# A long convolution and two gated layers on one core: PSUM laid out anew between stages, one product kept in PSUM, one fold on GpSimd

## The chip, the cores and the metric

The kernel runs on one core of a Trainium2 chip. The metric is device time in microseconds, the median of several runs. The engines are named as the profile names them: PE is TensorE (PEld is its weight load), DVE is VectorE, ACT is ScalarE, POOL is GpSimd, SP is SyncE, which here only issues DMAs. SBUF and PSUM are the two on-chip memories; PSUM has eight banks of 512 fp32 values in each of 128 partitions.

## The reference

Everything is fp32. A filter is made from `pos_emb`, `w1` and `w2`, windowed, and convolved along the sequence (12480 positions, 128 channels) with x times v, through a Fourier transform; the result, times x, goes through two two-layer networks.

```
h_filt = (relu(pos_emb @ w1) @ w2) * exp(-0.01 * pos)
y = irfft(rfft(x * v, 2S) * rfft(h_filt, 2S))[:S];  x = x * y
r = relu(x @ w_in);          x = (r * r) @ w_out
h = x @ w_in2;               out = (max(h, 0) + alpha * min(h, 0)) @ w_out2
```

## The kernel before

The transform of length 110 x 229 is done as two small ones with matmuls (`dfa` of 110, `dfb` of 229 folded to 115 rows). The channels are worked in two halves: h = 0, whose spectrum U(0) stands in the gaps of the big SBUF buffer G, and h = 1, whose spectrum U(1) fills the buffer R2. The work runs in stages, each a set of generators whose steps are interleaved by `run` (each generator has a weight, and the one that is least far along takes its next step). The code is written in this order, and each engine works through its own queue in it, waiting on semaphores:

- First stages (0 to 62.8 us): the filter (`z_stage`, `ar_stage`).
- Stage one (62.8 to about 136 us): `u_stage(0)` with `r_stage`. A step k of `u_stage` loads x and v, multiplies them on GpSimd two steps' worth ahead (`prep`, L251, two multiplies), transforms them (`u_mm_a`, L267 to L272) and, one step later, transforms again (`u_mm_b`, L280 to L287): two odd matmuls go to one PSUM bank and are copied to SBUF by ScalarE (L283), one even matmul goes to another bank, and VectorE writes even plus odd and even minus odd (L287, the two folds). `r_stage` makes the filter's tiles r and spills them.
- Stage two (about 136 to 236 us): `u_stage(1)`, 17 steps, with `p_stage(0)`, 14 steps.
- Stage three (236 to 299.4 us): `p_stage(1)`, 14 steps, with `b_stage(0)` (the inverse transform of half 0, L353, copied out by ScalarE, L361).
- After it: `b_stage(1)` (which reads U(1)), `y_stage`, and from 383 us on the two networks (`moe`), to the end. While these run, the networks' weights are decoded (`weights`, L437 to L454; L437 reads a PSUM bank and writes a PSUM bank).

A step of `p_stage` is a complex product of the spectrum with the filter for eight columns. For each of the parts c = 0 and c = 1, eight matmuls (L329) write a PSUM bank H, and VectorE multiplies U by H into the SBUF tile T (L334; half 0 in two instructions of 128 and 896 elements, half 1 in one of 1024). A is T's part 0, B its part 1. VectorE takes A's real half minus B's imaginary half (L341); one step later `finish` runs on GpSimd: A's imaginary half plus B's real half (L308), and the sums and differences that go back to U (L314). In the last step of each half VectorE does one of these two (also L314). All operands of L341, L308 and L314 are in SBUF. T is a ring of two.

PSUM is laid out once: eight tiles of one bank. Rings hand them out: `r_a` banks 0 and 1 (L267), `r_b` banks 2 to 4 (even and odd of `u_mm_b`), `r_h` banks 5 to 7 (H, and `r_stage`), `r_ab` banks 0 to 4 (`b_stage(0)`), `r_y` banks 0 to 5.

Of the kernel before, what the change touches and what calls it, by code (L numbers as in the profile page):

```python
# [9 lines left out]
F32 = mybir.dt.float32  # L10
# [5 lines left out]
ALU = mybir.AluOpType  # L16

S, D, F, FF = 12480, 128, 64, 2048
# [4 lines left out]
K2 = 2 * KA  # L23
HB = (NB + 1) // 2
# [7 lines left out]
DG = 4  # L32
# [18 lines left out]
def ring_of(pool, n, shape, dtype, name):  # L51
    return Ring(pool.tile(shape, dtype, name=f"{name}{i}") for i in range(n))
# [3 lines left out]
def kernel(  # L56
# [21 lines left out]
    nc = tc.nc  # L78
    PSUM = bass.MemoryType.PSUM
# [2 lines left out]
    dram = ctx.enter_context(tc.tile_pool(name="dram", bufs=1, space=bass.MemoryType.DRAM))  # L82
    s_g = ExitStack()
    p_g = s_g.enter_context(tc.tile_pool(name="p_g", bufs=1, side="right"))
    psum = ctx.enter_context(tc.tile_pool(name="psum", bufs=1, space=PSUM))
    banks = [psum.tile([128, 512], F32, name=f"bank{i}") for i in range(8)]
    r_any, r_a, r_b, r_h = Ring(banks), Ring(banks[0:2]), Ring(banks[2:5]), Ring(banks[5:8])
    r_ab, r_y = Ring(banks[0:5]), Ring(banks[0:6])

    def bank(ring, p, *dims):  # L90
        n = 1
        for d in dims:
            n *= d
        names = "uvwxyz"[:len(dims)]
        return ring()[:p, :n].rearrange(
            f"p ({' '.join(names)}) -> p {' '.join(names)}", **dict(zip(names, dims))
        )
# [160 lines left out]
        return bass.AP(tensor=v.tensor, offset=v.offset + HB - 1, ap=st)  # L258

    a_t = {}  # L260

    def u_mm_a(k):
        u = [t[:NA, :, 0:HB] for t in x_ring[k % NX][1:]]
# [10 lines left out]
    def u_mm_b(k):  # L274
        h, g = divmod(k, NG)
        a = a_t.pop(k)
        po = bank(r_b, HB, DG, 2, KA)
        pe = bank(r_b, HB, DG, K2)
        ao = a[:, 1].rearrange("p d (k c) -> p d k c", c=2)
        nc.tensor.matmul(po[:, :, 0], lhsT=nsinb, rhs=ao[:, :, :, 1])  # L280
        nc.tensor.matmul(po[:, :, 1], lhsT=sinb, rhs=ao[:, :, :, 0])
        t = t_ring[k % 2][:HB]
        nc.scalar.copy(out=t.rearrange("p d (k c) -> p d k c", c=2), in_=po.rearrange("p d c k -> p d k c"))  # L283
        nc.tensor.matmul(pe, lhsT=cosb, rhs=a[:, 0])  # L284
        u = U(h, 2 * DG * g, 2 * DG).rearrange("p (d s) k -> p d s k", s=2)
        for s, op in ((0, ALU.add), (1, ALU.subtract)):
            nc.vector.tensor_tensor(out=u[:, :, s], in0=pe, in1=t, op=op)  # L287

    def u_stage(h):
        for k in range(h * NG, (h + 1) * NG + 1):  # L290
            if k < (h + 1) * NG:
                load(k + NX - 1)
                u_mm_a(k)
                prep(k + NX - 3)
            if k > h * NG:
                u_mm_b(k - 1)
            yield
# [3 lines left out]
    p_order += [(j + nj - 6) % nj for j in range(nj)]  # L301

    def p_stage(h, t_ring, r_ring):
        late = []

        def finish(n, j, A, B):
            last = n % nj == nj - 1
            nc.gpsimd.tensor_tensor(out=A[:, :, :, 1], in0=A[:, :, :, 1], in1=B[:, :, :, 0], op=ALU.add)  # L308
            for x0, m in parts(h):
                y = A[:, x0:x0 + m].rearrange("p (d s) k c -> p d s (k c)", s=2)  # L310
                u = U(h, x0, m).rearrange("p (d s) k -> p d s k", s=2)[:, :, :, 8 * j:8 * j + 8]
                for s, op in ((0, ALU.add), (1, ALU.subtract)):
                    eng = nc.vector if last and s == 0 else nc.gpsimd
                    eng.tensor_tensor(out=u[:, :, s], in0=y[:, :, 0], in1=y[:, :, 1], op=op)  # L314

        for n in range(h * nj, (h + 1) * nj):
            j = p_order[n]
            m = p_order[min(n + 2, 2 * nj - 1)]
            if m not in r_t:
                del r_t[p_order[n - 1]]  # L320
                r_t[m] = r_ring()
                nc.sync.dma_start(out=r_t[m].rearrange("p q c k -> p (q c k)"), in_=spill[m])
            r = r_t[j]
            T = t_ring()
            for c in range(2):
                H = bank(r_h, HB, DH, 2, 2, 2)
                for q in range(2):
                    for s in range(2):
                        nc.tensor.matmul(  # L329
                            H[:, :, s, q], lhsT=r[:, q, 2 * s + c], rhs=w2_sb[:, h * D:(h + 1) * D]  # L330
                        )
                hv = H.rearrange("p d s q r -> p (d s) (q r)")
                for x0, m in parts(h):
                    nc.vector.tensor_tensor(  # L334
                        out=T[:, c, x0:x0 + m],
                        in0=U(h, x0, m)[:, :, 8 * j:8 * j + 8].rearrange("p x (k c) -> p x k c", c=2),
                        in1=hv[:, x0:x0 + m].unsqueeze(3).to_broadcast([HB, m, 4, 2]),
                        op=ALU.mult,
                    )
            A, B = T[:, 0], T[:, 1]  # L340
            nc.vector.tensor_tensor(out=A[:, :, :, 0], in0=A[:, :, :, 0], in1=B[:, :, :, 1], op=ALU.subtract)  # L341
            if late:
                late.pop()()
            late.append(lambda n=n, j=j, A=A, B=B: finish(n, j, A, B))
            yield
        late.pop()()

    def b_stage(h, alone):
        for g in range(NG):
# [64 lines left out]
    def run(*gens):  # L414
        live = [[g, n, i * 1e-6] for i, (g, n) in enumerate(gens)]
        while live:
            live.sort(key=lambda e: e[2])
            e = live[0]
            try:
                next(e[0])  # L420
                e[2] += 1.0 / e[1]
            except StopIteration:
                live.remove(e)
# [109 lines left out]
    n = NCH * NT  # L533
    i = j = 0
# [140 lines left out]
    with tc.manual_schedule():  # L675
        with ExitStack() as st:
            late = st.enter_context(tc.tile_pool(name="late", bufs=1))
            w2_sb = late.tile([128, 2 * D], F32, name="w2_sb")
            dfa = late.tile([NA, K2], F32, name="dfa")
            dfa_f = late.tile([NA, K2], F32, name="dfa_f")  # L680
            r_ring = ring_of(late, 3, [128, 2, 4, HB], F32, "r")
            with tc.tile_pool(name="early", bufs=1) as early:
                run((z_stage(*load_first(early)), 1))
                run((ar_stage(early), 1))
            with tc.tile_pool(name="rt", bufs=1) as rt:
                run((u_stage(0), NG + 1), (r_stage(rt, r_ring), KP))
            big = st.enter_context(tc.tile_pool(name="tt", bufs=1))
            tt = ring_of(big, 2, [HB, 2, D, 4, 2], F32, "T")
            p0, q0 = p_stage(0, tt, r_ring), p_stage(1, tt, r_ring)
            run((u_stage(1), NG + 1), (p0, nj + 1))  # L690
            run((q0, nj + 3), (b_stage(0, False), NG))
        wa = ctx.enter_context(tc.tile_pool(name="wa", bufs=1))
        wst = ctx.enter_context(tc.tile_pool(name="wst", bufs=1))
        decode = weights(wst)
# [179 lines left out]
```

## Time and profile before

| | |
|---|---|
| median of 3 runs | 1478.89 us (1477.95 to 1481.53) |
| profiled execution | 1478.57 us, span 1476.8 us |
| PE busy in the span | 1441.3 us (98%) |
| DVE, POOL, ACT busy | 80%, 71%, 65% |
| mean granted TensorE clock | 0.992 |

The page's shares are means over stages with different limits. From 306 us on PE is busy in every slice, and the chain that ended last runs through PE's matmuls; the change touches none of that work. What it touches lies between 62 and 300 us, so the rows below are taken from there. A row of a timeline merges instructions that follow each other on an engine; behind it stands, in brackets, the idle time before it and who ended it.

### The profile page before, as it was taken

Reading aid. Unit: us, or ns where it says so; the run is one execution under the profiler, and the core shown is the slowest. Engines: PE = TensorE matmul, PEld = TensorE weight load, DVE = VectorE, ACT = ScalarE, POOL = GpSimd, SP = SyncE. Lnnn points to the kernel's source line nnn. Section 1 sums busy time; section 2 is a strip of 40 time slices with the busy share of each in tenths; the row PEclk is TensorE's granted clock in tenths of the full one; section 3 lists DMA queues with packets and bytes.
Section 4 is the critical chain, followed back from the end, with each engine's and each line's share of the span. In section 5 each row is a group of like instructions: output and inputs, shape, how many; then the busy total and the mean of one; then the engine's idle time right before and its main releaser. Section 6 shows DMA issues by size and latency. Waiting matters only on the chain.

```text
span 1476.8 us, 23093 instructions
## 1 busy us (share of the span) xinstructions
PE 1441.3 (98%) x7634; PEld 1231.4 (83%) x7634; DVE 1174.6 (80%) x1852; ACT 966.9 (65%) x1857; POOL 1042.9 (71%) x851
## 2 busy tenths in 40 slices
PE   8999888889999999999999999999999999999998
PEld 8989778789888888888888888888888888888887
DVE  5978998769778877777777777777777787777998
ACT  5333112262588777777777777777777777777776
POOL 2245998944677777777777777777777777777766
PEclk9999989999999999999999999999999999999999
DMA  9388922239600000000000000000000000000000
GB/s 285 94 217 230 211 84 78 65 106 278 205 22 8 1 8 8 1 8 8 8 8 8 7 2 8 7 8 8 8 1 8 8 8 8 8 8 1 15 15 14
DMA packets 73869, 76.83 MB, mean 52 GB/s; under 512 B 6739, under 2 KB 65428, under 8 KB 73364
## 3 DMA queue, kind: packets, MB, share of 16 engines
q1 hardware_dynamic: 72650, 71.12, 17.4%
q0 software_dynamic: 688, 3.93, 0.8%
q8 instruction: 60, 0.98, 0.3%
q14 instruction: 62, 0.50, 0.1%
q10 hardware_dynamic: 409, 0.29, 0.1%
HBM read 58.41 MB, written 16.92 MB: 51 GB/s over the span
## 4 chain that ended last, share of the span: by engine, by line
PE 89%; POOL 5%; DVE 3%; issue 2%; DMA 1%; ACT 0%; POOLq 0%; DVEq 0%; ACTq 0%
PE bank L565 24%; PE bank L566 24%; PE bank L567 24%; PE bank L267 3%; PE bank L353 2%; PE bank L168 2%; PE bank L407 2%; PE bank L406 2%; DVE R L205 2%; PE bank L223 2%; POOL R L314 2%; POOL T L308 2%; PE bank L284 1%; PE bank L329 1%; PE bank L280 1%
## 5 line engine op out<-in xcount | busy, mean ns | idle before, releaser
L618 POOL TENSOR_TENSOR g<-R,g 128x500 fp32r<-128x500 f32 (+1 forms) x598 | 776.9, 1320 | 279.6 <-ACT g L607 204.2
L600 DVE SCALAR_TENSOR_TENSOR R<-bank,e 128x500 f32<-128x500 f32 (+1 forms) x800 | 531.4, 674 | 172.3 <-POOL g L618 95.4
L607 ACT CAST g<-R 128x500 fp32r<-128x500 f32 (+1 forms) x800 | 466.3, 604 | 32.3 <-DVE R L600 28.4
L585 ACT ACTIVATE e<-bank 128x500 f32<-128x500 f32 (+1 forms) x400 | 234.7, 587 | 165.2 <-PE bank L567 162.1
L590 DVE TENSOR_SCALAR e<-bank,alpha 128x500 f32<-128x500 f32 (+1 forms) x266 | 195.3, 734 | 50.4 <-PE bank L567 50.1
L618 DVE TENSOR_TENSOR g<-R,g 128x500 fp32r<-128x500 f32 (+1 forms) x202 | 158.2, 784 | 0.0
L566 PE MATMUL bank<-g,w_o 128*128 128x500 f32 (+1 forms) x400 | 155.7, 389 | 0.4 <-POOL g L618 0.4
L567 PE MATMUL bank<-g,w_o 128*128 128x500 f32 (+1 forms) x400 | 155.5, 389 | 0.0
L566 PE MATMUL bank<-x,w_i 128*128 128x500 f32 (+1 forms) x400 | 155.4, 388 | 0.0
L565 PE MATMUL bank<-x,w_i 128*128 128x500 f32 (+1 forms) x400 | 155.2, 388 | 0.0
L565 PE MATMUL bank<-g,w_o 128*128 128x500 f32 (+1 forms) x400 | 155.0, 388 | 0.0
L567 PE MATMUL bank<-x,w_i 128*128 128x500 f32 (+1 forms) x400 | 155.0, 387 | 0.0
L567 PE MATMUL bank<-g,w_o0b 128*128 128x500 f32 (+1 forms) x350 | 136.4, 390 | 0.0
L566 PE MATMUL bank<-g,w_o0b 128*128 128x500 f32 (+1 forms) x350 | 136.3, 389 | 0.0
L565 PE MATMUL bank<-g,w_o0b 128*128 128x500 f32 (+1 forms) x350 | 135.7, 388 | 0.0
L251 POOL TENSOR_TENSOR G<-G 110x460 f32<-110x460 f32 x64 | 73.9, 1174 | 86.7 <-DMA G<-in_vs_dram 49.3
L587 ACT ACTIVATE e<-bank 128x500 f32<-128x500 f32 (+1 forms) x134 | 78.8, 588 | 39.3 <-PE bank L567 38.6
L588 ACT ACTIVATE e<-e,alpha 128x500 f32<-128x500 f32 (+1 forms) x134 | 95.6, 714 | 4.4
L566 PEld LDWEIGHTS bank<-x,w_i 128*128 128x128 f32 x400 | 75.1, 188 | 15.9
L566 PEld LDWEIGHTS bank<-g,w_o 128*128 128x128 f32 x400 | 75.2, 188 | 15.8 <-POOL g L618 0.8
L565 PEld LDWEIGHTS bank<-x,w_i 128*128 128x128 f32 x400 | 75.3, 188 | 15.6
L565 PEld LDWEIGHTS bank<-g,w_o 128*128 128x128 f32 x400 | 75.2, 188 | 15.4
(107 smaller groups left out, 2632.1 us busy)
## 6 DMA issues: line engine op xcount, KB each, us to landing
G<-in_vs_dram SPq DMA_DIRECT2D x64, 224.0 KB, 5.5
r<-spill SPq DMA_DIRECT2D x22, 460.0 KB, 4.2
G<-in_xs_dram SPq DMA_DIRECT2D x32, 224.0 KB, 5.4
spill<-r SPq DMA_DIRECT2D x14, 460.0 KB, 3.0
out_dram<-R SPq DMA_DIRECT2D x24, 250.0 KB, 2.0
R<-in_xt_dram SPq DMA_DIRECT2D x27, 218.0 KB, 3.8
s_w<-in_moe_w_in_dram SPq DMA_DIRECT2D x16, 256.0 KB, 3.4
s_w<-in_moe_w_out_dram SPq DMA_DIRECT2D x16, 256.0 KB, 3.6
```

What stands on the lines that cost most here:

```text
L251: nc.gpsimd.tensor_tensor(out=u[:, :, 0:HB], in0=u[:, :, 0:HB], in1=y, op=ALU.mult)
L267: nc.tensor.matmul(p[s][:, d], lhsT=u[s][:, d], rhs=dfa)
L565: nc.tensor.matmul(p, lhsT=wl, rhs=xh, start=first, stop=False)
L566: nc.tensor.matmul(p, lhsT=wh, rhs=xl, start=False, stop=False)
L567: nc.tensor.matmul(p, lhsT=wh, rhs=xh, start=False, stop=last)
L585: nc.scalar.activation(out=r, in_=p, func=ACTF.Relu)
L587: nc.scalar.activation(out=r, in_=p, func=ACTF.Relu, scale=-1.0)
L588: nc.scalar.activation(out=r, in_=r, func=ACTF.Copy, scale=alpha[:, t:t + 1])
L590: nc.vector.tensor_scalar(out=r, in0=p, scalar1=0.0, scalar2=alpha[:, t:t + 1], op0=ALU.min, op1=ALU.mult)
L600: nc.vector.scalar_tensor_tensor(out=g, in0=p, scalar=0.0, in1=r, op0=ALU.max, op1=op)
L607: nc.scalar.copy(out=gh, in_=g)
L618: eng.tensor_tensor(out=gl, in0=g, in1=gh.bitcast(F32), op=ALU.subtract)
```

## The change

- PSUM is laid out three times. `lay_banks` closes the pool of PSUM tiles and opens another: eight tiles for the first stages and stage one; then, for stages two and three, six tiles of one bank and one tile `wide` of two banks; then eight tiles again. In stages two and three `r_b` and `r_h` shrink from three banks to two, and `r_ab` from five to four.
- In `p_stage` the c = 1 product B is written to `wide` in PSUM instead of SBUF. The tile A alone is the ring of two in SBUF. Real and imaginary part are now both finished on VectorE (L356 of the new code), and GpSimd's addition L308 is gone. `finish` comes at the end of its own step instead of one step later.
- In `u_mm_b` the even matmul comes first. In stage two (h = 1) ScalarE copies its bank to a new SBUF tile `even`, and the second fold (even minus odd) goes to GpSimd; in stage one both folds stay on VectorE.

```diff
@@ lay_banks
+    def lay_banks(name, n):
+        s_psum.close()
+        pool = s_psum.enter_context(tc.tile_pool(name=name, bufs=1, space=PSUM))
+        tiles = [pool.tile([128, 512], F32, name=f"{name}{i}") for i in range(n)]
+        if n < 8:
+            tiles.append(pool.tile([128, (8 - n) * 512], F32, name=f"{name}_wide"))
+        return tiles
@@ u_mm_b
+        pe = bank(r_b, HB, DG, K2)
         po = bank(r_b, HB, DG, 2, KA)
-        pe = bank(r_b, HB, DG, K2)
+        nc.tensor.matmul(pe, lhsT=cosb, rhs=a[:, 0])
+        even = None
+        if h:
+            even = even_ring[0]()
+            nc.scalar.copy(out=even, in_=pe)
...
-        nc.tensor.matmul(pe, lhsT=cosb, rhs=a[:, 0])
...
-        for s, op in ((0, ALU.add), (1, ALU.subtract)):
-            nc.vector.tensor_tensor(out=u[:, :, s], in0=pe, in1=t, op=op)
+        nc.vector.tensor_tensor(out=u[:, :, 0], in0=pe, in1=t, op=ALU.add)
+        if h:
+            nc.gpsimd.tensor_tensor(out=u[:, :, 1], in0=even, in1=t, op=ALU.subtract)
+        else:
+            nc.vector.tensor_tensor(out=u[:, :, 1], in0=pe, in1=t, op=ALU.subtract)
@@ p_stage, finish
-            nc.gpsimd.tensor_tensor(out=A[:, :, :, 1], in0=A[:, :, :, 1], in1=B[:, :, :, 0], op=ALU.add)
@@ p_stage
-            T = t_ring()
-            for c in range(2):
+            A = t_ring()
+            B = wide[:HB].rearrange("p (x k c) -> p x k c", k=4, c=2)
+            for c, out_c in enumerate((A, B)):
...
-                        out=T[:, c, x0:x0 + m],
+                        out=out_c[:, x0:x0 + m],
...
-            A, B = T[:, 0], T[:, 1]
-            nc.vector.tensor_tensor(out=A[:, :, :, 0], in0=A[:, :, :, 0], in1=B[:, :, :, 1], op=ALU.subtract)
-            if late:
-                late.pop()()
-            late.append(lambda n=n, j=j, A=A, B=B: finish(n, j, A, B))
+            for c, op in ((0, ALU.subtract), (1, ALU.add)):
+                nc.vector.tensor_tensor(out=A[:, :, :, c], in0=A[:, :, :, c], in1=B[:, :, :, 1 - c], op=op)
+            finish(n, j, A)
@@ between stages
+            *few, wide = lay_banks("pb", 6)
+            r_a.items, r_b.items, r_h.items, r_ab.items = few[0:2], few[2:4], few[4:6], few[0:4]
-            tt = ring_of(big, 2, [HB, 2, D, 4, 2], F32, "T")
+            tt = ring_of(big, 2, [HB, D, 4, 2], F32, "T")
+            even_ring.append(ring_of(big, 2, [HB, DG, K2], F32, "even"))
...
+        banks = lay_banks("bank", 8)
+        r_y.items = banks[0:6]
```

GpSimd's queue at the start of stage two, before (T is the product's tile, G holds x, v and U(0)):

```order
L251 TENSOR_TENSOR G<-G 110x4x115 x42
L308 TENSOR_TENSOR T_1102<-T_1102 115x512
L314 TENSOR_TENSOR G<-T_1102 115x8x8 x2
L314 TENSOR_TENSOR G<-T_1102 115x56x8 x2
L251 TENSOR_TENSOR G<-G 110x4x115 x2
L308 TENSOR_TENSOR T_1103<-T_1103 115x512
L314 TENSOR_TENSOR G<-T_1103 115x8x8 x2
```

And now (L260 is `prep`, L328 the finish, L302 the new fold, which writes U(1) in R):

```order
L260 TENSOR_TENSOR G<-G 110x4x115 x40
L328 TENSOR_TENSOR G<-T_1113 115x8x8 x2
L328 TENSOR_TENSOR G<-T_1113 115x56x8 x2
L260 TENSOR_TENSOR G<-G 110x4x115 x2
L302 TENSOR_TENSOR R_78<-even_1115,G 115x4x112
L328 TENSOR_TENSOR G<-T_1114 115x8x8 x2
L328 TENSOR_TENSOR G<-T_1114 115x56x8 x2
```

A step now holds two multiplies, one fold and four finishing instructions, where it held L308, four finishing instructions and two multiplies; one pair of multiplies moved behind the first finish.

VectorE's queue in one step of stage two, before (L272 makes a, L287 is the two folds into R, L334 the products):

```order
L272 TENSOR_TENSOR G<-G,bank_70 115x4x112 x2
L287 TENSOR_TENSOR R_78<-bank_71,G 115x4x112 x2
L334 TENSOR_TENSOR T_1103<-G,bank_74 115x128
L334 TENSOR_TENSOR T_1103<-G,bank_74 115x896
L334 TENSOR_TENSOR T_1103<-G,bank_75 115x128
L334 TENSOR_TENSOR T_1103<-G,bank_75 115x896
L341 TENSOR_TENSOR T_1103<-T_1103 115x512
```

And now (L282 makes a, L300 is the one fold left, L349 the products, pb are the new banks):

```order
L282 TENSOR_TENSOR G<-G,pb_1104 115x4x112 x2
L300 TENSOR_TENSOR R_78<-pb_1105,G 115x4x112
L349 TENSOR_TENSOR T_1114<-G,pb_1107 115x128
L349 TENSOR_TENSOR T_1114<-G,pb_1107 115x896
L349 TENSOR_TENSOR pb_wide<-G,pb_1108 115x128
L349 TENSOR_TENSOR pb_wide<-G,pb_1108 115x896
L356 TENSOR_TENSOR T_1114<-T_1114,pb_wide 115x512 x2
```

One fold went to GpSimd and one L356 came; every instruction shown has a PSUM operand, where L341 had none.

PE's queue where stage one ends and stage two begins, with the semaphores that each row waits for, before (bank_69 and bank_70 are the ring `r_a`):

```order
L284 MATMUL bank_72<-G,dfb 115x448 [waits Activation_49]
L223 MATMUL bank_74<-dfb,R_78 128x115 x4
L267 MATMUL bank_69<-dfa,G 115x112 [waits DMAHW3_49,Pool_49]
L267 MATMUL bank_69<-dfa,G 115x112 x3
L267 MATMUL bank_70<-dfa,G 115x112 [waits DMAHW4_49,Pool_49]
```

And now:

```order
L296 MATMUL bank_72<-G,dfb 115x4x56
L232 MATMUL bank_74<-dfb,R_78 128x115 [waits Activation_49]
L232 MATMUL bank_74<-dfb,R_78 128x115 x3
L277 MATMUL pb_1103<-dfa,G 115x112 [waits DVE_49,DMAHW3_49,Activation_49,Pool_49]
L277 MATMUL pb_1103<-dfa,G 115x112 x3
```

The first matmul into the new layout waits for VectorE as well: for the last instruction that reads a tile of the old one (L239 of the new code, L230 of the old).

## Rows read from the trace of the kernel before

**Rows 1.** Busy time by stretch: us, us long, engines' busy us, PEclk, DMA share, GB/s.
```profile
100.00:136.00 36.00, 36.00 (x269) 31.80 (x268) 26.81 (x57) 13.08 (x29) 18.42 (x16) 1.00 0.84 218
136.00:236.00 100.00, 88.14 (x603) 76.68 (x602) 96.48 (x141) 17.38 (x33) 89.25 (x90) 0.91 0.57 136
236.00:299.40 63.40, 50.71 (x465) 48.54 (x463) 46.38 (x43) 17.46 (x32) 59.91 (x41) 1.00 0.27 83
300.00:306.00 6.00, 6.00 (x34) 6.00 (x34) 1.54 (x4) 1.75 (x4) 0.45 (x1) 0.52 0.58 94
```

**Rows 2.** Timeline of DVE and POOL in one step of stage two.
```profile
147.06 2.27 POOL L251 TENSOR_TENSOR G<-G 110x460 f32<-110x460 f32 x2
...
147.42 2.46 DVE L341 TENSOR_TENSOR T<-T 115x512 f32<-115x512 f32 x1
...
149.30 1.95 POOL L308 TENSOR_TENSOR T<-T 115x512 f32<-115x512 f32 x1
149.81 1.14 DVE L272 TENSOR_TENSOR G<-G,bank 115x448 f32<-115x448 f32 x2
...
150.87 1.15 DVE L287 TENSOR_TENSOR R<-bank,G 115x448 f32<-115x448 f32 x2
...
151.33 2.78 POOL L314 TENSOR_TENSOR G<-T 115x64 f32<-115x64 f32 x4
...
151.93 2.47 DVE L334 TENSOR_TENSOR T<-G,bank 115x128 f32<-115x128 f32 x4
...
154.04 2.31 POOL L251 TENSOR_TENSOR G<-G 110x460 f32<-110x460 f32 x2
```

**Rows 3.** Timeline where stage one ends and stage two begins.
```profile
136.73 1.77 PE L267 MATMUL bank<-dfa,G 110*115 110x112 f32 x16
...
137.67 0.39 DVE L230 TENSOR_TENSOR r<-bank,rt 128x230 f32<-128x230 f32 x1
...
142.18 0.69 DVE L341 TENSOR_TENSOR T<-T 115x512 f32<-115x512 f32 x1
```

**Rows 4.** Timeline from the end of stage two into stage three.
```profile
232.45 0.65 PE L280 MATMUL bank<-G,dfb 115*115 115x224 f32 x2 [1.60 <-DVE G L272]
...
233.34 0.91 PE L284 MATMUL bank<-G,dfb 115*115 115x448 f32 x2
233.38 1.42 DVE L314 TENSOR_TENSOR G<-T 115x64 f32<-115x64 f32 x2
...
235.97 2.35 DVE L334 TENSOR_TENSOR T<-R,bank 115x1024 f32<-115x1024 f32 x2
...
238.35 0.69 DVE L341 TENSOR_TENSOR T<-T 115x512 f32<-115x512 f32 x1
...
238.96 2.35 DVE L334 TENSOR_TENSOR T<-R,bank 115x1024 f32<-115x1024 f32 x2
```

**Rows 5.** Timeline of POOL in stage three.
```profile
243.39 1.52 POOL L308 TENSOR_TENSOR T<-T 115x512 f32<-115x512 f32 x1
244.98 2.95 POOL L314 TENSOR_TENSOR R<-T 115x512 f32<-115x512 f32 x2
```

**Rows 6.** Timeline of DVE and PE at the end of stage three.
```profile
290.48 4.92 PE L353 MATMUL bank<-dfb,G 115*112 115x116 f32 x48
...
298.64 0.69 DVE L314 TENSOR_TENSOR R<-T 115x512 f32<-115x512 f32 x1 [2.59 <-POOL T L308]
...
299.48 6.73 PE L353 MATMUL bank<-dfb,R 115*112 115x116 f32 x35 [4.08 <-DVE R L314]
```

**Rows 7.** Four lines' instructions: count, duration in ns (min/median/max), first and last start, form.
```profile
L205 DVE TENSOR_TENSOR R<-ar_p,bank x32: 911/937/953, 35.0 to 61.8; 115x448 f32<-115x448 f32 x32
L283 ACT COPY G<-bank x32: 532/532/533, 67.3 to 233.6; 115x448 f32<-115x448 f32 x32
L270 ACT COPY G<-bank x32: 532/532/533, 61.5 to 228.6; 115x448 f32<-115x448 f32 x32
L437 DVE TENSOR_SCALAR bank<-bank x32: 415/424/433, 304.3 to 487.4; 128x256 f32<-128x256 f32 x32
```

More of the change, by code (lines that the diff above doesn't have):

```diff
@@ L84 @@
     p_g = s_g.enter_context(tc.tile_pool(name="p_g", bufs=1, side="right"))
-    psum = ctx.enter_context(tc.tile_pool(name="psum", bufs=1, space=PSUM))
-    banks = [psum.tile([128, 512], F32, name=f"bank{i}") for i in range(8)]
+    s_psum = ctx.enter_context(ExitStack())
+    def lay_banks(name, n):
[6 more added lines that the diff above has]
+    banks = lay_banks("bank", 8)
     r_any, r_a, r_b, r_h = Ring(banks), Ring(banks[0:2]), Ring(banks[2:5]), Ring(banks[5:8])
-    r_ab, r_y = Ring(banks[0:5]), Ring(banks[0:6])
+    r_ab, r_y = Ring([]), Ring([])
     def bank(ring, p, *dims):
@@ L260 @@
     a_t = {}
+    even_ring = []
     def u_mm_a(k):
@@ L303, in p_stage, with finish @@
     def p_stage(h, t_ring, r_ring):
-        late = []
-        def finish(n, j, A, B):
+        def finish(n, j, A):
             last = n % nj == nj - 1
-            nc.gpsimd.tensor_tensor(out=A[:, :, :, 1], in0=A[:, :, :, 1], in1=B[:, :, :, 0], op=ALU.add)
             for x0, m in parts(h):
@@ L339, in p_stage @@
                     )
-            A, B = T[:, 0], T[:, 1]
-            nc.vector.tensor_tensor(out=A[:, :, :, 0], in0=A[:, :, :, 0], in1=B[:, :, :, 1], op=ALU.subtract)
-            if late:
-                late.pop()()
-            late.append(lambda n=n, j=j, A=A, B=B: finish(n, j, A, B))
+            for c, op in ((0, ALU.subtract), (1, ALU.add)):
+                nc.vector.tensor_tensor(out=A[:, :, :, c], in0=A[:, :, :, c], in1=B[:, :, :, 1 - c], op=op)
+            finish(n, j, A)
             yield
-        late.pop()()
     def b_stage(h, alone):
@@ L691 @@
             run((q0, nj + 3), (b_stage(0, False), NG))
+        banks = lay_banks("bank", 8)
+        r_y.items = banks[0:6]
         wa = ctx.enter_context(tc.tile_pool(name="wa", bufs=1))
```

## The prediction

> **What bounds the kernel now.** The page's chain of waits comes first: from 306 us on it is PE's matmuls, without a gap worth counting, and nothing there changes. So the question is how much earlier the work after stage three can start, and every microsecond won before 299.48 us [rows 6] should be one won at the end. The busy times by stretch come next [rows 1]. In stage one PE is busy 36.00 of 36 us, VectorE 26.81: PE bounds it. In stage two VectorE shows 96.48 and GpSimd 89.25 of 100, PE 88.14 at a granted clock of 0.91. In stage three GpSimd shows 59.91 of 63.4, PE 50.71, VectorE 46.38.
>
> The timeline of one step of stage two says what the two full engines really do [rows 2]. The step is 6.98 us long (L251 at 147.06 and 154.04). L341 takes 2.46 us, while the same instruction takes 0.69 where GpSimd is idle [rows 3, 4]. It starts at 147.42 inside GpSimd's pair of multiplies, which runs to 149.30, and ends 0.58 after that, at 149.88: it stood still until GpSimd was through. Then GpSimd's L308, issued at 149.30, takes 1.95 us instead of the 1.52 in stage three [rows 5]: it stood still until L341 was through. L272, L287 and L334, which take one operand from PSUM, run beside GpSimd at full pace: L334's four instructions take 2.47 beside L314. So VectorE's 96 us hold about 1.8 us of standing still in most of 14 steps, and the step's length is GpSimd's: 2.24 for L251, 2.03 for L308 (to the start of L314), 2.71 for L314. In stage three GpSimd alone sets the step: L308 and two L314, 1.52 + 2.95, about 4.5, times 14 is the stretch of 63.4 us.
>
> **Part by part. Stage two, GpSimd.** L308 goes; one fold of 115x448 comes. Its price is that of one multiply of 460 elements, 1.12 us [rows 2]; the bounds are 1.09 (448 of its 460 elements) and L308's 1.52. A step is then 2.24 + 1.12 + 2.71 = 6.1 us.
> **Stage two, VectorE.** One fold goes (0.53, half of the spacing 149.81 to 151.93 less L272's 1.06), L341 stays without its stall, and a second such instruction comes. Both L356 take one operand from PSUM, so by rows 2 they don't meet GpSimd. Two L341 follow at 0.61 (238.35 to 238.96) [rows 4], so the step is L282 1.06, L300 0.53, products 2.5, L356 1.22, together 5.3, with waits on its own results 5.4. GpSimd remains the longer one. Where L356 reads `wide` it takes every second fp32 value; no row shows VectorE reading PSUM so. The lower bound is 0.69; the upper one is L205, 937 ns for 448 elements, which jumps in SBUF and in PSUM [rows 7]: scaled from L334 (2.35 for 2048 elements, about 1.05 ns each and 0.14 fixed) it is 1.8 ns per element, so 1.05 us for 512. I take 0.69: L283 reads PSUM on ScalarE with jumps, and takes the same 532 ns as L270 without [rows 7]; L205's extra time can come from its SBUF side. The products that now go to PSUM: L437 writes PSUM at 424 ns for 256 elements [rows 7], which is 0.14 + 256 x 1.05 = 0.41 and so no dearer than SBUF; the upper bound is again 1.8 ns each, 1.95 in place of 1.2. I take 1.2.
>
> The Trainium skill, "Advanced Engine Details and Errata", section "PSUM Cachelines", speaks against this: PSUM lines hold two fp32 values, and both should be used for best throughput. By it each L356 would be at its upper bound, and the sum would be rival B's. L283's 532 ns says that on ScalarE it does not hold here; no row shows VectorE.
>
> **Stage two's start.** The new PSUM layout makes PE wait for the last reader of the old one. Before, PE began stage two at 136.73, while L230 ended at 138.06 [rows 3]. With the even matmul first, the folds of stage one come some 0.4 later, so PE begins at 138.5; the first products start at 141.4 and the first complex product ends at 145.1, where L341 ended at 142.87. That is a loss of 2.2 us, paid once. In stage one itself the later fold is hidden: VectorE has 9 us of 36 free [rows 1], and PE waits for that bank a step later. Without that cover it would be 0.4 x 16 = 6 us.
>
> **Stage two's length.** GpSimd: first finish 145.1 to 147.8; seven steps of 6.1 to 190.5; one step of `u_stage` alone (multiplies and fold, 3.4) to 193.9; four more steps to 218.3. The last product needs the tile that this frees, so VectorE starts it at 218.3: products and L356 to 222.0, its share of the last finish (1.42 [rows 4]) to 223.4, L282 and the fold before the last to 225.0. Then one chain that cannot overlap: three matmuls (232.45 to 234.25 before, 1.8) [rows 4], ScalarE's copy 0.53, GpSimd's fold 1.12, waits 0.1: 228.5. Only then may stage three's first product start, which was at 235.97 [rows 4]. Gain 7.5. From VectorE's sum alone (141.4 + 14 x 5.4 and the tail) it would be some 226, a gain of 10; the copies of `even` (16 x 0.53) lie in ScalarE's idle time, 17 of 100 us busy [rows 1]. PE's clock fell to 0.91 because PE waited; with less waiting it should rise, and PE has 5 us to do in 6.1.
>
> **Stage three.** VectorE: 2.38 (235.97 to 238.35) + 1.22 = 3.6 us a step; GpSimd's two L328 need at most 2.95 [rows 5]; PE has 50.71 us for the stage [rows 1]. Fourteen steps of 3.62 are 50.7, the last fold 0.7: 51.4, against 63.4 before. Gain 12.0. H has two banks instead of three: the next c = 1 matmuls wait for this step's second product, which ends 1.2 us before the step does; that is enough for their 0.9. Without it a step would be longer by some 0.3.
>
> **After it.** Before, PE had run its last 48 matmuls of `b_stage(0)` to 295.40 and then waited 4.08 us for U(1) [rows 6]; after that its granted clock was 0.52 until 306 us, that is the 1.2 GHz level for nearly 6 us, which costs half of them [rows 1]. Now U(1) is ready 14 x 3.62 + 0.7 after the stage's start, and PE's last 4.92 us end at about the same time. Gain 2.7, or nothing if PE still waits 4 us.
>
> Sum: 7.5 + 12.0 + 2.7 = 22.2 from the profiled execution's 1478.57 us: 1456.4. That execution lies 0.3 below the median of 1478.89, so 1456.7; I say 1457.
>
> **Rivals.** B, the stride costs: L356 at 1.05. VectorE's step in stage two is 6.1 and stage two wins 3.7; stage three has 4.36 a step and wins 1.6; with the clock's 2.7 that is 8: 1471. For it: L205. Against: L283.
> C, stage two gives nothing: waits that the rows can't show (matmuls behind the two-bank rings, PE at half clock after short waits, GpSimd's fold queued behind ScalarE, with the four finishing instructions behind it) eat the 7.5. Stage three and the clock stay: 14.7, so 1464. For it: three engines each within 20% of the bound. Against: GpSimd's 6.1 rests on rows.
> D, the standing still remains, because L356 or the products, with a PSUM operand, still meet GpSimd: a step of stage two with multiplies is then 5.4 + 1.8 = 7.2; twelve of them lose 0.2 each, the start 2.2 and the closing chain some 1.4, in all 6; stage three keeps about 10, the clock 2.7: 1472. Against: L272, L287 and L334 run beside GpSimd unharmed.
> E, slower: `wide` costs at both ends, 1.95 for the product that writes it and 1.05 for each L356. Stage three's step is 3.62 + 0.73 + 0.73 = 5.08, 72 us, a loss of 8.5; stage two's is 6.9 on VectorE and loses 8; PE waits before U(1) as it did. 1495. It decides from about 0.85 us more per step in stage three on, where 4.5 is reached. Against: L437.
>
> **How the numbers follow.** Forecast 0.58, its own range 1452 to 1462; B 0.15, C 0.14, D 0.04, E 0.05, and 0.04 for a mixture that comes out near no change. This kernel can be measured to about 0.3%, 4.4 us; what lies closer counts as the same, so 1474.5 to 1483.3. B's and D's upper edges fall there too: faster 0.86, same 0.08, slower 0.06. The range reaches from the forecast's lower edge (stage two by VectorE's sum alone, 1454, and 2 us for steps that overlap better) past B and D: 1452 to 1473.
>
> **What would show it.** On VectorE: L356 near 0.69 in both stages, none near 2.4; the c = 1 product as long as the c = 0 one. On GpSimd: 6.1 between pairs of multiplies, no finishing instruction prolonged. PE's first matmul of stage two some 1.7 us later than VectorE would have allowed before; stage three's first product at 228 to 229; about 3.6 us between products in stage three, with GpSimd idle a quarter of it; U(1) at 280 and PE at full clock there. L356 at 1.05 makes it B; a c = 1 product near 2 us makes it E and the forecast wrong; a first product of stage three near 236 with L356 at 0.69 makes it C.

## The result, and the profile after

The changed kernel takes 1461.82 us (median of 4 executions, 1461.5 to 1462.22) against 1478.42 in the same comparison: the ratio is 0.9887, with a 95% interval of 0.9875 to 0.9899. The forecast was 1457, with a range of 1452 to 1473. The profiled execution of the changed kernel takes 1461.5 us, its span is 1459.5, so 17.1 us less than the one of before, where 22.2 were forecast. The four stretches of [rows 1], now of the changed kernel:

```profile
100.00:136.00 36.00, 36.00 (x270) 32.16 (x269) 25.65 (x57) 12.54 (x28) 16.12 (x14) 1.00 0.80 217
136.00:236.00 100.00, 85.88 (x619) 75.20 (x618) 87.47 (x141) 26.29 (x52) 81.52 (x94) 0.93 0.64 140
236.00:299.40 63.40, 62.72 (x586) 60.69 (x585) 56.59 (x76) 26.50 (x55) 38.82 (x34) 1.00 0.37 106
300.00:306.00 6.00, 6.00 (x63) 6.00 (x62) 4.67 (x12) 5.18 (x13) 3.53 (x5) 1.00 0.38 107
```

PE fills stage one as before. The second row holds all of stage two and the first 2.5 us of stage three; no engine fills it: VectorE is busy 87.47, GpSimd 81.52 of 100, and PE's granted clock rose only from 0.91 to 0.93. The third is full on PE, and in the last the granted clock is 1.00 instead of 0.52. The start of stage two, as in [rows 3] (timeline: start, length, engine, line; in brackets the idle time before it and what ended it):

```profile
138.59 1.84 PE L277 MATMUL pb<-dfa,G 110*115 110x112 f32 x16 [1.74 <-DVE r L239]
...
141.60 1.28 DVE L349 TENSOR_TENSOR T<-G,pb 115x128 f32<-115x128 f32 x2
...
144.25 1.29 DVE L356 TENSOR_TENSOR T<-T,pb_wide 115x512 f32<-115x512 f32 x2
```

PE waits 1.74 us for L239, the last reader of the old layout, and the first complex product ends at 145.54, 2.7 later than before. One step of stage two on VectorE and GpSimd, as in [rows 2]:

```profile
148.25 1.42 DVE L349 TENSOR_TENSOR pb_wide<-G,pb 115x128 f32<-115x128 f32 x2
148.41 2.29 POOL L260 TENSOR_TENSOR G<-G 110x460 f32<-110x460 f32 x2
...
149.70 1.29 DVE L356 TENSOR_TENSOR T<-T,pb_wide 115x512 f32<-115x512 f32 x2
...
150.68 1.13 POOL L302 TENSOR_TENSOR R<-even,G 115x448 f32<-115x448 f32 x1
150.90 1.14 DVE L282 TENSOR_TENSOR G<-G,pb 115x448 f32<-115x448 f32 x2
...
151.77 2.76 POOL L328 TENSOR_TENSOR G<-T 115x64 f32<-115x64 f32 x4
...
154.50 1.17 POOL L260 TENSOR_TENSOR G<-G 110x460 f32<-110x460 f32 x1
```

L356 starts inside GpSimd's pair of multiplies, where L341 stood still before, and now both of its instructions are through in 1.29. GpSimd's step, from 148.41 to 154.50, is 6.09. The 56 instructions of L356 in both stages (one line of the profile: count, ns as minimum, median and maximum, first and last start):

```profile
L356 DVE TENSOR_TENSOR T<-T,pb_wide x56: 673/685/695, 144.3 to 283.2; 115x512 f32<-115x512 f32 x56
```

None stands still, and reading every second value of PSUM costs nothing (L341 took 0.69 with both inputs in SBUF, [rows 3, 4]). The end of stage two, as in [rows 4]:

```profile
218.76 1.09 DVE L349 TENSOR_TENSOR T<-G,pb 115x896 f32<-115x896 f32 x1 [0.54 <-POOL G L328]
...
222.41 1.22 POOL L302 TENSOR_TENSOR R<-even,G 115x448 f32<-115x448 f32 x1
222.54 4.14 DVE L328 TENSOR_TENSOR G<-T 115x64 f32<-115x64 f32 x2
223.50 1.48 POOL L328 TENSOR_TENSOR G<-T 115x64 f32<-115x64 f32 x2
224.85 1.22 POOL L302 TENSOR_TENSOR R<-even,G 115x448 f32<-115x448 f32 x1
226.61 1.14 DVE L282 TENSOR_TENSOR G<-G,pb 115x448 f32<-115x448 f32 x2
227.67 0.61 DVE L300 TENSOR_TENSOR R<-pb,G 115x448 f32<-115x448 f32 x1
...
228.34 1.84 PE L289 MATMUL pb<-G,dfb 115*115 115x448 f32 x2 [8.15 <-DVE R L300]
...
229.97 0.95 PE L295 MATMUL pb<-G,dfb 115*115 115x224 f32 x2
...
230.72 0.95 PE L296 MATMUL pb<-G,dfb 115*115 115x224 f32 x2
...
232.31 1.14 POOL L302 TENSOR_TENSOR R<-even,G 115x448 f32<-115x448 f32 x1 [6.25 <-ACT G L298]
233.48 1.22 DVE L349 TENSOR_TENSOR T<-R,pb 115x1024 f32<-115x1024 f32 x1 [0.59 <-POOL R L302]
```

Here are the missing microseconds. VectorE's share of the last finishing step, two small instructions, takes 4.14 us instead of 1.42: the first of them, over 115x64, lasts 3608 ns of it (below), and ends at 226.15, just after GpSimd's last queued instruction (224.85 + 1.22 = 226.07). It did not wait for that instruction's result: the L302 at 224.85 is the second fold of the group whose first fold, the L300 at 227.67, stands behind it in VectorE's own queue. L282 and L300 for the last group are queued behind VectorE's stalled instruction, PE waits 8.15 for them, and then runs its three pairs of matmuls at half pace: the pair of L289 takes 1.84, in the middle of the stage 0.92 (L284 in [rows 4], which is the same pair, 0.91). The line of VectorE's two instructions:

```profile
L328 DVE TENSOR_TENSOR G<-T x2: 609/2108/3608, 222.5 to 226.1; 115x64 f32<-115x64 f32 x1, 115x448 f32<-115x448 f32 x1
```

The granted clock of the stretch in which PE takes up work again (the columns of [rows 1]):

```profile
228.30:231.50 3.20, 3.17 (x7) 2.05 (x8) 0.00 (x0) 0.53 (x1) 0.00 (x0) 0.50 0.00 0
```

0.50 is the 1.2 GHz level. Stage three begins at 233.48. One of its steps on VectorE with the start of the next, and GpSimd's part beside it, against [rows 5]:

```profile
262.22 1.21 DVE L349 TENSOR_TENSOR T<-R,pb 115x1024 f32<-115x1024 f32 x1
263.35 1.22 DVE L349 TENSOR_TENSOR pb_wide<-R,pb 115x1024 f32<-115x1024 f32 x1
264.60 1.29 DVE L356 TENSOR_TENSOR T<-T,pb_wide 115x512 f32<-115x512 f32 x2
265.81 1.22 DVE L349 TENSOR_TENSOR T<-R,pb 115x1024 f32<-115x1024 f32 x1
```

```profile
262.38 2.50 POOL L328 TENSOR_TENSOR R<-T 115x512 f32<-115x512 f32 x2 [1.10 <-DVE T L356]
```

A step is 3.59, set by VectorE; GpSimd waits 1.1 in each; the product that writes PSUM is as fast as the one that writes SBUF. The end of stage three, as in [rows 6]:

```profile
283.87 0.69 DVE L328 TENSOR_TENSOR R<-T 115x512 f32<-115x512 f32 x1
```

```profile
279.95 4.92 PE L365 MATMUL pb<-dfb,G 115*112 115x116 f32 x48
285.56 25.61 PE L365 MATMUL bank<-dfb,R 115*112 115x116 f32 x256 [0.68 <-issue]
```

PE goes on after 0.68 us, at full clock (1.00 from 300 to 306 us, the fourth stretch above), where it waited 4.08 before. The difference of the two spans can now be added up from rows. U(1) is ready at 284.56 instead of 299.33: 14.8, of which 2.5 were won up to stage three's first product (235.97 to 233.48) and 12.3 in stage three. PE starts on it 1.00 after it is ready instead of 0.15: minus 0.85. From that start to the end of the span it was 1476.8 - 299.48 = 1177.3 before, and is 1459.5 - 285.56 = 1173.9 now, 3.4 shorter. Together 17.3, and the spans differ by 1476.8 - 1459.5 = 17.3.

### The profile page after: what moved, and what is told of

The parts are those of the page before. It is cut to its first block, busy times and chain, and to the rows that moved or that the text cites. A ratio compares the mean times of both kernels' runs of the same rounds, so it can differ in the third digit from the quotient of the medians.

```text
span 1459.5 us, 23117 instructions
## 1 busy us (share of the span) xinstructions
PE 1433.7 (98%) x7634; PEld 1225.5 (84%) x7634; DVE 1161.1 (80%) x1864; ACT 973.7 (67%) x1873; POOL 1005.5 (69%) x839
## 4 chain that ended last, share of the span: by engine, by line
PE 88%; DVE 5%; issue 3%; POOL 2%; ACT 1%; DMA 1%; POOLq 0%; DVEq 0%; ACTq 0%
PE bank L577 24%; PE bank L578 24%; PE bank L579 24%; PE bank L177 2%; PE bank L419 2%; PE bank L418 2%; DVE R L214 2%; PE bank L232 2%; PE bank L277 2%; PE pb L344 1%; DVE pb_wide L349 1%; PE pb L277 1%; PE bank L289 1%; DVE T L356 1%; DMA G<-in_vs_dram 1%
## 5 line engine op out<-in xcount | busy, mean ns | idle before, releaser
L619 ACT CAST g<-R 128x500 fp32r<-128x500 f32 (+1 forms) x800 | 466.0, 604 | 27.4 <-DVE R L612 24.6
L630 DVE TENSOR_TENSOR g<-R,g 128x500 fp32r<-128x500 f32 (+1 forms) x202 | 154.3, 764 | 0.0
L260 POOL TENSOR_TENSOR G<-G 110x460 f32<-110x460 f32 x64 | 73.8, 1177 | 84.6 <-DMA G<-in_vs_dram 75.4
```

The costliest lines, as they stand in the source:

```text
L260: nc.gpsimd.tensor_tensor(out=u[:, :, 0:HB], in0=u[:, :, 0:HB], in1=y, op=ALU.mult)
L619: nc.scalar.copy(out=gh, in_=g)
L630: eng.tensor_tensor(out=gl, in0=g, in1=gh.bitcast(F32), op=ALU.subtract)
```

## The experiments

The comparisons were run against the kernel before, which took 1478.02 (first four), 1479.27 (next four) and 1479.43 (last three); beside the changed kernel it took 1478.42. The same kernel thus differs by up to 1.4 us between the comparisons, and medians of runs from different ones are compared no finer than that. All edits but the first are to the changed kernel.

**layout_alone.** The kernel before with the PSUM layouts of the change and nothing else:

```diff
+            *few, wide = lay_banks("pb", 6)
+            r_a.items, r_b.items, r_h.items, r_ab.items = few[0:2], few[2:4], few[4:6], few[0:4]
...
+        banks = lay_banks("bank", 8)
+        r_y.items = banks[0:6]
```

> The kernel before with the new layouts of PSUM alone: eight tiles, then six and an unused pair, then eight; products, finishing and folds as they were. Theory (the prediction's): the barrier between the layouts costs once, at the start of stage two (first matmul of stage two near 138.5 instead of 136.73), and rings of two banks cost no step anything: 1480.5 us, between 1479 and 1483. Rival: rings of two banks make PE wait in every step of stage two, by half a microsecond or more, and of stage three: 1487 or more, first product of stage three after 241.

Measured: 1479.59, ratio 1.0011 (1.0001 to 1.002). Two rows of its timeline, PE at the start of stage two and VectorE at the start of stage three:

```profile
139.22 1.83 PE L276 MATMUL pb<-dfa,G 110*115 110x112 f32 x16 [1.42 <-DVE r L239]
```

```profile
238.52 2.35 DVE L343 TENSOR_TENSOR T<-R,pb 115x1024 f32<-115x1024 f32 x2
```

Stage three starts 2.5 later than in [rows 4], and by the medians the whole costs 1.6, just clear of the noise. The delay is there from the start and does not grow: VectorE's first product of stage two comes at 142.23 instead of 139.67, 2.6 later. Of it 0.9 are stage one's end, whose last matmuls came later in this execution (136.75 for 135.85), and 1.6 the barrier, paid once. Rings of two banks cost no step anything. The first theory holds.

**folds_on_vector.** Both folds on VectorE again; the imaginary product stays in `wide`:

```diff
-        if h:
+        if False:
             even = even_ring[0]()
             nc.scalar.copy(out=even, in_=pe)
...
-        if h:
+        if False:
             nc.gpsimd.tensor_tensor(out=u[:, :, 1], in0=even, in1=t, op=ALU.subtract)
```

> The changed kernel with both folds on VectorE from PSUM, no copy of the even part, no fold on GpSimd; the imaginary product stays in the wide PSUM tile. VectorE's step of stage two grows by half of the pair's spacing, 0.53, to 5.97; GpSimd's falls to 2.3 + 2.75 = 5.0. Theory 1 (VectorE's finishing instructions at the end of stage two stand still behind GpSimd's closing instructions, 3.6 us instead of 0.3, and GpSimd's folds are what keeps it full there): here the 14 steps end at 141.6 + 83.6 = 225.2, the finishing share takes 1 to 1.5, the last fold is done near 233, first product of stage three 232 to 234: 1460 to 1463, no different from the changed kernel. Theory 2 (the fold on GpSimd carries stage two's gain): 0.53 times 16 is lost, 1469 to 1471, first product near 241.

Measured: 1466.32, ratio 0.9917 (0.9902 to 0.9932), 4.5 above the changed kernel, between what the two theories gave. VectorE at the end of stage two:

```profile
229.68 0.88 DVE L328 TENSOR_TENSOR G<-T 115x64 f32<-115x64 f32 x2
...
238.01 1.22 DVE L349 TENSOR_TENSOR T<-R,pb 115x1024 f32<-115x1024 f32 x1
```

The same two finishing instructions take 0.88 here, with no queue on GpSimd in front of them, so the first theory has its stall right. Its sum was wrong, and with it the time: products come every 5.97 us as worked out, but the one step that has a group and no product takes 5.0 more (184.85 to 195.83 between two products), and the stage started 1.4 later in that execution. The fold on GpSimd is worth 4.5 us as it stands.

**b_in_sbuf.** As folds_on_vector, with the imaginary product in SBUF:

```diff
-            A = t_ring()
-            B = wide[:HB].rearrange("p (x k c) -> p x k c", k=4, c=2)
+            T = t_ring()
+            A, B = T[:, 0], T[:, 1]
```

> As folds_on_vector, but the imaginary product stays in SBUF beside the real one, as in the kernel before; both combining instructions on VectorE, each with two operands in SBUF. Theory (a VectorE instruction with two SBUF inputs stands still while GpSimd runs back to back): in stage two the two combining instructions meet GpSimd's 5 us of work per step and stand still 1 to 2 us a step, 14 to 28 us; in stage three they follow a gap of GpSimd and lose at most 0.3 a step: 1475 to 1495, single instructions of 2 us and more in the trace. Rival (the place of the operand does not matter): as folds_on_vector within 2 us, all of them 0.69.

Measured: 1470.63, ratio 0.9944 (0.9929 to 0.9959): 4.3 above folds_on_vector, far less than the 14 to 28 expected, and more than the rival's 2. L356 over both stages, then a step of stage two on GpSimd and on VectorE:

```profile
L356 DVE TENSOR_TENSOR T<-T x56: 676/689/1174, 145.8 to 291.9; 115x512 f32<-115x512 f32 x56
```

```profile
162.45 2.31 POOL L260 TENSOR_TENSOR G<-G 110x460 f32<-110x460 f32 x2
```

```profile
164.21 1.71 DVE L356 TENSOR_TENSOR T<-T 115x512 f32<-115x512 f32 x2
```

The pair takes 1.71 instead of 1.29. The stall is there, but it is 0.42: L356 comes at 164.21, when GpSimd's pair (162.45 to 164.76) is nearly through, and GpSimd's finishing instructions cannot start before L356 is done. Each step falls into this phase again. A step is 6.26 instead of 5.97, so 0.29 longer and not 0.42: the four products up to L356 take 2.50 here (161.71 to 164.21) and 2.64 in folds_on_vector (160.95 to 163.59), where the second pair writes PSUM. In the kernel before, L341 came 0.4 after the pair's start and lost 1.8 [rows 2]. So the theory's mechanism holds and its size does not: the price is what is left of GpSimd's run when VectorE comes.

**last_finish_on_gpsimd.** VectorE takes no share of stage two's last finishing step:

```diff
-                    eng = nc.vector if last and s == 0 else nc.gpsimd
+                    eng = nc.vector if last and s == 0 and h else nc.gpsimd
```

> The changed kernel with one edit: VectorE takes no share of the last finishing step of stage two; GpSimd does all four instructions. Theory 1 (the VectorE instruction of 115x64 that takes 3.6 us at 222.54 holds the last stage-one multiplies and folds up, PE waits 8.15 us for them and then runs at half its clock): the last L282 starts at 222.6 instead of 226.61, the last fold on GpSimd ends near 229, first product of stage three at 229 to 230 instead of 233.48: 1456 to 1458. Theory 2 (the closing chain itself, PE at the lower clock and GpSimd's queue, sets the end): GpSimd has 1.4 us more in front of its last fold, and the first product moves by less than 1.5: 1460 to 1463.

Measured: 1458.99 (1457.65 to 1460.05), ratio 0.9864 (0.9848 to 0.9881), 2.8 below the changed kernel. VectorE at the end of stage two, in the execution profiled:

```profile
224.47 1.15 DVE L282 TENSOR_TENSOR G<-G,pb 115x448 f32<-115x448 f32 x2
...
231.35 1.22 DVE L349 TENSOR_TENSOR T<-R,pb 115x1024 f32<-115x1024 f32 x1 [0.59 <-POOL R L302]
```

The median lies between the times of the two theories, so the rows have to decide. The first product of stage three comes at 231.35, only 2.1 earlier and not at 229 to 230. But this execution (1460.05, the longest of the four) lost 2.0 at the start of stage two: GpSimd's first finishing instruction is at 147.72 instead of 145.68. From there to stage three's first product it is 83.6 us instead of 87.8: 4.2 won, what the first theory said. Of the 2.0 at the start, 0.7 are stage one's last matmuls, which came later (136.46 for 135.81), and 1.3 are PE's clock: after the same wait of 1.74 for the old layout's last reader, its first 16 matmuls take 3.17 instead of 1.84:

```profile
139.20:142.40 3.20, 3.16 (x17) 3.19 (x18) 0.00 (x0) 0.53 (x1) 0.00 (x0) 0.55 0.81 242
```

The closing chain is as dear as in the changed kernel. PE waits 3.99 for L300 instead of 8.15 and runs at half pace all the same; from the end of L300 (226.16) to stage three's first product it is again 5.2:

```profile
226.21 1.84 PE L289 MATMUL pb<-G,dfb 115*115 115x448 f32 x2 [3.99 <-DVE R L300]
```

**one_layout.** One pool of six tiles and a pair from the start; the pair's halves stand in for the seventh and eighth bank:

```diff
+    wide = psum.tile([128, 1024], F32, name="wide")
+    banks = few + [wide[:, 0:512], wide[:, 512:1024]]
```

> The changed kernel with one layout of PSUM from the start (six tiles and a pair, the pair's halves serving as the seventh and eighth bank outside stages two and three): no barrier between layouts, all else the same. Theory (the prediction's term of the start): PE begins stage two near 136.8 instead of 138.59 and does not drop to the lower clock, the first complex product ends 1.7 to 3.5 earlier, stage two ends as much earlier: 1458 to 1460.5. Rival (the start is hidden behind the loads, or GpSimd's sum absorbs it): 1461.5 to 1462.5, first product of stage three still at 233 to 234.

Measured: 1522.17, ratio 1.0292 (1.0277 to 1.0308). Slower than either kernel, and both theories missed it, because the edit did something else as well. PE's waits of the whole execution (line, waited for, us in total, times, longest):

```profile
PE wide L570 <- ACT R L643: 17.8, 24, 2.5
...
PE wide L203 <- DVE R L207: 7.6, 4, 1.9
PE wide L225 <- DVE r L232: 6.5, 4, 1.6
```

PE waits at tile `wide` in the first stages, in stage one and in the networks, wherever a ring changes between the halves; the changed kernel's list has none of these. In stage one, whose ring hands out the two halves one after the other, PE's write to the one (104.44) waits for VectorE's read of the other (L232, 103.91 to 104.30). So two slices of one tile serve as one buffer in this program. PE's waits at `wide` come to 37 of the 60 us by which the span is longer; the rest was not taken apart. The run says nothing of the barrier.

**closing.** The last product behind the last fold, and no share of VectorE in the last finishing step:

```diff
-            run((u_stage(1), NG + 1), (p0, nj + 1))
+            run((u_stage(1), NG + 1), (p0, nj - 1))
```

> The changed kernel with the last product of stage two put behind the last fold (the product stage paced by 13 instead of 15 in 17 steps of the stage that folds), and VectorE takes no share of the last finishing step. Theory 1 (after the changed kernel's stage two 5 us are lost in the closing chain: VectorE stands still, PE waits 8 us and then runs at half clock for three matmuls): the last product now covers that chain, PE waits less than 2 us there, and stage three's first product is at 226 to 228 instead of 233.48: 1454 to 1456.5. Theory 2 (GpSimd's sum, 6.1 us a step, is what sets the end): its last fold comes at 228 or later, first product 229 to 231: 1457 to 1459.5.

Measured: 1458.22, ratio 0.9861 (0.9845 to 0.9877), 3.6 below the changed kernel. VectorE where stage three begins:

```profile
227.54 1.29 DVE L356 TENSOR_TENSOR T<-T,pb_wide 115x512 f32<-115x512 f32 x2
228.74 1.21 DVE L349 TENSOR_TENSOR T<-R,pb 115x1024 f32<-115x1024 f32 x1
```

The chain is covered: VectorE passes from the last product of one stage to the first of the next without a gap, 4.7 earlier than in the changed kernel. It is just later than the first theory's 226 to 228, because VectorE, not GpSimd, now ends the stage; the time lies in the second theory's range, but GpSimd's last fold began at 227.23 and was in time. How much of this is the finishing step alone? By the medians, 2.8 in last_finish_on_gpsimd and 3.6 here, the two can't be told apart. By the rows, from GpSimd's first finishing instruction (145.95 here) to stage three's first product it is 82.8, where it was 83.6 and, in the changed kernel, 87.8. So 4.2 of these 5.0 are the finishing step's, and laying the last product over the chain adds 0.8.

**closing_mix.** As closing, with every third group's second fold on VectorE:

```diff
-        if h:
+        if h and k % 3:
```

> As closing, and every third group's second fold (six of 16) on VectorE from PSUM instead of on GpSimd. GpSimd's sum falls by 6 times 1.13, 6.8 us, VectorE's rises by 6 times 0.53, 3.2 us. Theory (both engines are within a few us of each other over stage two, GpSimd the longer): VectorE becomes the longer one, stage three's first product comes 2 to 4 earlier than in closing: 1451 to 1454. Rival (VectorE was as full as GpSimd already): no earlier or later by up to 3: 1455 to 1459.

Measured: 1457.79, ratio 0.9856 (0.9842 to 0.9871), the same as closing; the first product of stage three is at 228.68. The rival's number came, but its reason did not: VectorE was not full. Five folds of 0.53, 2.7 us, were added to it, and within the stage its waits fell from 7.8 us in closing to 4.6. So neither engine's sum alone sets the end of this stage. (Of the groups 16 to 31 five, not six, are multiples of three; the sums of the expectation shrink by a sixth.)

**all_four.** closing_mix with one_layout.

> closing_mix and one layout together. If the two gains are independent, closing_mix less what one_layout gains over the changed kernel: 1448 to 1452; if the barrier's loss is hidden, as closing_mix within 1 us.

Measured: 1519.38, ratio 1.0273 (1.0258 to 1.0289): spoiled as one_layout was.

**two_pools.** Six tiles that stay through the whole kernel; only the last two banks are laid out anew:

```diff
+    few = [psum.tile([128, 512], F32, name=f"bank{i}") for i in range(6)]
+    banks = few + lay_pair("pair", 2)
...
-            *few, wide = lay_banks("pb", 6)
+            wide, = lay_pair("pw", 1)
...
-        banks = lay_banks("bank", 8)
+        banks = few + lay_pair("pair", 2)
```

> The changed kernel with six PSUM tiles that stay through the whole kernel, and only the last pair of banks laid out anew (two tiles, one double tile, two tiles). All else the same. Theory (the prediction's start term, freed of what spoiled one_layout): PE's first matmul of stage two no longer waits for the last reader of the old layout, so it starts near 136.8 instead of 138.59 and at full clock; stage three's first product 1.5 to 3.5 earlier than 233.48: 1458 to 1460.5. Rival (start hidden): 1461.5 to 1462.5.

Measured: 1460.46 (1459.92 to 1461.25), ratio 0.9873 (0.9856 to 0.9889), 1.4 below the changed kernel. PE at the start of stage two, and VectorE at its end:

```profile
136.70 1.04 PE L231 MATMUL bank<-dfb,R 115*128 115x115 f32 x8
137.57 1.77 PE L276 MATMUL bank<-dfa,G 110*115 110x112 f32 x16
```

```profile
221.44 4.15 DVE L327 TENSOR_TENSOR G<-T 115x64 f32<-115x64 f32 x2
...
232.39 1.22 DVE L348 TENSOR_TENSOR T<-R,bank 115x1024 f32<-115x1024 f32 x1 [0.59 <-POOL R L301]
```

PE passes from stage one into stage two with no wait, and stage three's first product comes 1.1 earlier, or 2.0 if it is counted from stage one's last matmuls, which came 0.9 later in this execution (136.70 for 135.81). The medians alone don't show it: the two intervals overlap. VectorE's stall at the end is there again: 4.15, after 4.14.

**closing_two.** closing on the six lasting tiles.

> closing with the six lasting tiles of two_pools. If both gains are independent: closing's 1458.2 less 1.5 to 3: 1455 to 1456.7. If the engine that bounds stage two is GpSimd and its first work comes as late as before: 1458.

Measured: 1454.78 (1454.36 to 1455.13), ratio 0.9833 (0.9819 to 0.9848): 24.6 below the kernel before and 7.0 below the changed one. It is the fastest version here, and lies just below the first theory's 1455 to 1456.7. Stage three's first product on VectorE:

```profile
227.13 1.22 DVE L348 TENSOR_TENSOR T<-R,bank 115x1024 f32<-115x1024 f32 x1
```

The stretch in which the last chain and the last product lie beside each other (the columns of [rows 1]):

```profile
219.00:228.00 9.00, 6.26 (x41) 5.13 (x42) 8.86 (x14) 1.07 (x2) 6.89 (x11) 1.00 0.00 1
```

VectorE is busy 8.86 of 9 us and PE's granted clock is 1.00, where it was 0.50 in the closing chain of the changed kernel.

**mix_two.** closing_two with every third second fold on VectorE.

> closing_two, and every third group's second fold on VectorE. In closing_mix this shift of 6.8 us of GpSimd's work to 3.2 us of VectorE's moved nothing (1457.8 against 1458.2), so VectorE's sum bounds stage two once the closing chain is covered: again as closing_two within 1 us. If GpSimd bounds once the start is earlier: 1453 to 1454.5.

Measured: 1456.92, ratio 0.9848 (0.9834 to 0.9863), 2.1 above closing_two; the first product of stage three is at 229.50. Both theories missed it. Five folds of 0.53, 2.7 us, were added to VectorE, but that they are the reason is not shown: in closing_mix the same five cost nothing. Of the 2.4 by which the first product is later, 2.2 arise in one step, the one without a product (178.83 to 189.84 between two products, 177.76 to 186.58 in closing_two). In it PE waited 1.95 and then had a granted clock of 0.53 (184.0 to 187.5), where in closing_two it waited 1.43 and kept 1.00. Which of the two cost it is open.

## Why the prediction was right, and where 5 us went

**The shape was right.** Stage one did not change (PE 36.00 of 36). The two combining instructions with one operand in PSUM run beside GpSimd at 0.69 in each of 56 cases; the product into PSUM takes 1.22 against 1.21; GpSimd's step is 6.09 (6.1 forecast), stage three takes 51.1 (51.4), U(1) no longer keeps PE waiting and PE's clock stays up there (3.4 won from the start on U(1) on, less 0.85 for that start, so 2.5; 2.7 forecast). Rivals B, D and E are out by the line of L356 and the two lines of L349. Against B, the rule of the Trainium skill, "Advanced Engine Details and Errata", section "PSUM Cachelines", that PSUM lines want both their values used, does not hold for these VectorE reads: 685 ns with every second value, 0.69 in SBUF.

**How near it was.** The median lies in the forecast's own range, 1452 to 1462, by 0.2 us, and nearer to rival C's 1464 than to 1457. The sign set for C, a first product of stage three near 236 with L356 at 0.69, came by two thirds: 233.48, where the forecast had 228.5. One of C's reasons, PE at half clock after waits, is part of what follows; another, rings of two banks, cost no step anything in layout_alone.

**The start was right**, and a little dearer: PE at 138.59 (138.5), the first complex product at 145.54 (145.1). layout_alone shows it alone, 1.6 us; two_pools takes it away, 2.0 by its rows (1.4 by medians of two comparisons, within their spread).

**GpSimd's sum was right** to half a microsecond, the half of the start: seven steps to 190.95 (190.5), the single step to 194.29 (193.9), VectorE's last product at 218.76 (218.3).

**The step that failed is the end of stage two**: "its share of the last finish (1.42 [rows 4]) to 223.4", and "Then one chain that cannot overlap: three matmuls (232.45 to 234.25 before, 1.8)". Both durations were carried over from the kernel before, where they had other neighbours and PE the full clock. The finishing share took 4.14: 2.7 more. From the end of L300 (228.28) to stage three's first product it took 5.2 instead of 3.5: 1.7 more, of which 1.5 are the three pairs of matmuls, 3.3 at the 1.2 GHz level (228.34 to 231.67) instead of 1.8. With the 0.5 from the start that is 4.9 of the 5.0 by which the first product came late (233.48 for 228.5), and so nearly all of the difference between 22.2 and 17.1. Stage two won 2.5 instead of 7.5.

The reason was at hand in the prediction's own reading. L328 has both inputs in SBUF, as L341 had; the prediction used that to explain L341's standing still and let L356 out of the danger, without asking which other instruction of this kind stays on VectorE. One did, at the end, and it met a GpSimd whose queue had become full without gaps: that queue is what the change itself brought. Even the 1.42 of before held some half a microsecond of it, as 0.88 in folds_on_vector shows. The rule behind it is in the Trainium skill, "SBUF — State Buffer", section "Who interferes with whom": VectorE with two SBUF inputs contends with a GpSimd instruction that reads SBUF, with at most one, outside its two-port modes, it doesn't. The traces agree (685 ns for L356 in every place, 3.6 us for L328). Where the section says how long the shared ports are held, it is of those modes, and for one whole instruction; here VectorE stood through all that GpSimd had queued, four instructions from 222.41 on.

That VectorE's finishing share cost what its row says is shown by last_finish_on_gpsimd (4.2 won within the stage without it) and, from the other side, by folds_on_vector (0.88 with GpSimd's queue empty) and two_pools, where the 4.15 came again. The chain's half clock was not tried alone. It does not hang on the long wait of 8.15: the chain is as dear after the 3.99 of last_finish_on_gpsimd. In the kernel before, PE waited 1.60 there [rows 4] and had the full clock (1.00 from 228 to 238 us). What taking the chain away is worth is not 1.7 either: closing lays the last product over it and wins 0.8 by its rows, because VectorE then ends the stage.

**The parts of the gain**, from the medians, one edit after another: the layouts lose 1.6; both combining instructions on VectorE, with the even part's matmul first and the finishing not held back a step, win 9.0 (1479.59 to 1470.63); the imaginary product in PSUM wins 4.3 more; the fold on GpSimd 4.5 more.

## To carry to other kernels

When an engine's queue is filled up, look for every instruction on the other engine that shares a resource with it, above all the rare ones at a stage's end: their price is not their length but what is left in the queue. A closing chain is priced with the clock and the neighbours that it will have then, and laying the last independent piece of work over it pays as far as the engine that does this work has time left: 0.8 us here. A new layout of PSUM waits for the last reader only where it must: tiles that need not move are better kept.

## What the runs showed that was not expected

- VectorE's instruction over 115x64 stood 3.6 us, through four GpSimd instructions in a row, and ended 0.08 after the last; in two_pools it was the same, 4.15 for the two. GpSimd's run was not broken for it.
- The same stall cost 0.42 a step in b_in_sbuf and 1.8 in the kernel before, by the phase in which the two engines fell.
- A wait of PE of 1.74 us at the barrier was followed by full clock in the profiles of the changed kernel, folds_on_vector, b_in_sbuf, closing and closing_mix (1.84 for the first 16 matmuls in each) and by a granted clock of 0.55 for some 3 us in that of last_finish_on_gpsimd: the same wait, two prices.
